# Filter twiddles by one vector product and a sum in PSUM, and a smaller last store, in a long-convolution kernel

## The chip, the cores and the metric

The kernel runs on one core of one Trainium2 chip. The metric is the device time of one execution in microseconds (us). The core has a matrix engine (TensorE, in the profile PE, its weight loads PEld), a vector engine (VectorE, DVE), an activation engine (ScalarE, ACT), GpSimd (POOL) and SyncE (SP), which here only issues transfers. ACT and POOL issue transfers as well. Each engine works through its own instructions in order and waits on semaphores; the transfers run beside them on 16 DMA engines that all queues share.

## The reference, cut to what matters

Batch 4, sequence 12800, width 128, filter order 64, all in float32:

```python
h_filt = (np.maximum(pos_emb @ w1, 0.0) @ w2) * np.exp(-0.01 * pos)[:, None]
u = x * v
y = np.fft.irfft(np.fft.rfft(u, n=2 * S, axis=1) * np.fft.rfft(h_filt, n=2 * S, axis=0)[None], n=2 * S, axis=1)[:, :S]
a = x * y                                   # gated long convolution
gate = 1 / (1 + np.exp(-depthwise_conv5(a)))  # causal, 5 taps
out = (gate * (a @ w_val)) @ w_out
```

The three small weights of the last line come in as float64.

## The kernel before, in words

The convolution of length 25600 is done as a two-step Fourier transform: a position is split into j (2 halves), n1 (100) and n2 (64), and a frequency into k1 (100) and k2 (64). The program has three phases, and each hands its result to the next through device memory.

**Phase 1** (lines 209 to 427) makes two things. The *signal* part is a generator, `signal()`: for each of 64 values of n it multiplies x by v, forms sums and differences on DVE (`prep`, lines 324 to 345, lines 319 to 338 in the profile), transforms over n1 with matmuls (tile `fp`, line 387), copies the result from PSUM to a tile `st` on ACT (line 388), and stores that to the array `a_u` in device memory. It yields after each of the two halves (`c`) of an n, so it has 128 half steps. The inputs come by SP into a ring of nine buffers (`fetch`); when the matmuls of a pair of n have read their buffers, `release` loads them anew. One n reads 0.82 MB and writes 0.82 MB.

The store of an n has three parts by k1 (`PARTS`, line 32): rows k1 = 0 to 63 on the ACT queue, 64 to 95 on the POOL queue (both line 394), and 96 to 99 on the POOL queue one n later (line 407).

The *filter* part is a second generator, `filt()`, with three kinds of step:

- 34 steps that transpose `pos_emb`, multiply by w1 and write the windowed, rectified result to `g_sb` (lines 229 to 254);
- 32 steps `ap` (lines 261 to 272): matmuls that transform `g_sb` over n1, and an ACT copy into `ag`;
- 26 steps `fk`/`gp` (lines 274 to 293): for four k1 at a time, `turned` makes four twiddled 128 x 128 matrices. For each k1, ACT writes sine times one table, and DVE adds cosine times another table to it in place (line 279). A matmul per k1 then multiplies `ag` by the matrix (line 289), and ACT copies the four results back into `ag` (line 291). The first of the 26 steps only makes the first matrices.

The two generators are interleaved by a list of due times, `due` (lines 411 to 414), counted in n; after each half step of the signal, all filter steps that are due are issued. The order in which the lines run is the order in which each engine gets its instructions (`manual_schedule`). Before the change the 34 steps are due from n = 3 on, each half an n apart, to 19.5; the 32 steps from 20 to 36.5; the 26 steps from 36.5 to 63.

**Phase 2** (lines 454 to 589) runs over 50 pairs p of k1 (p holds k1 = 2p and 2p + 1). For each pair the 128 rows of `a_u` at these two k1 are loaded (`load_a`, line 201), transformed over n2 (`z_ps`, line 482), multiplied by the filter's spectrum (`times`, line 488, tiles va, vb, vc, vd on DVE) and transformed back; results go to `c_y` and `c_z`. Pairs 0 and 1 are loaded in pieces: `EARLY` holds the rows of n = 0 to 55, `LATE` those of n = 56 to 63 (line 188). The `EARLY` rows of pair 0 are loaded from the POOL queue at n = 61, and those of pair 1 at n = 63; the `LATE` rows by SP at the start of phase 2. The tiles of phase 2 lie in pools `p2` and `ps2`, in memory that phase 1 held before.

**Phase 3** (lines 599 to 825) finishes the inverse transform, multiplies by x, and does the five taps, the gate and the two projections. The change does not touch it.

Of the kernel before, what the change touches and what calls it, by code (L numbers as in the profile page):

```python
# [9 lines left out]
F32 = mybir.dt.float32  # L10
F32R = mybir.dt.float32r
I32 = mybir.dt.int32
AF = mybir.ActivationFunctionType
ALU = mybir.AluOpType
PSUM = bass.MemoryType.PSUM
# [8 lines left out]
B, S, D, FO, KC = 4, 12800, 128, 64, 5  # L24
J, N1, N2 = 2, 100, 64
# [92 lines left out]
def tile_longconv_gate(  # L118
# [20 lines left out]
    nc = tc.nc  # L139
# [15 lines left out]
    dft = const.tile([128, 2, 2 * N2], F32, name="dft")  # L155
# [53 lines left out]
    with tc.tile_pool(name="p1", bufs=1) as p1, tc.tile_pool(name="ps1", bufs=1, space=PSUM) as ps1:  # L209
        pos_v = pos.rearrange("(j a n) f -> j a n f", j=J, a=N1)  # L210

        g_sb = p1.tile([N1, J, N2, FO], F32, name="g_sb")

        HC = 16

# [8 lines left out]
        def filt():  # L224
# [47 lines left out]
                yield  # L272

            def turned(k0):
                fk = p1.tile([128, 4, 2 * N2], F32, name="fk", bufs=2)
                for i in range(4):
                    k1 = k0 + i
                    nc.scalar.activation(fk[:, i], dft[:, 1], AF.Copy, scale=tw[:, 1, k1:k1 + 1])
                    nc.vector.scalar_tensor_tensor(
                        fk[:, i], dft[:, 0], tw[:, 0, k1:k1 + 1], fk[:, i], op0=ALU.mult, op1=ALU.add)  # L280
                return fk

            fk = turned(0)
# [1 line left out]
            for k0 in range(0, N1, 4):  # L285
                following = turned(k0 + 4) if k0 + 4 < N1 else None
                gz = ps1.tile([128, 4, 2 * N2], F32, name="gp", bufs=1)
                for i in range(4):
                    nc.tensor.matmul(
                        out=gz[:, i], lhsT=ag[:, k0 + i].rearrange("p j e -> p (j e)"), rhs=fk[:, i], start=True, stop=True)  # L290
                nc.scalar.copy(out=ag[:, k0:k0 + 4].rearrange("p k j e -> p k (j e)"), in_=gz)
                fk = following
                yield
# [59 lines left out]
        def signal():  # L353
            fetch(4)
            load_pos(0)
            fetch()
            load_pos(HC)
            ready = [prep(0)]
            for n in range(N2):
                if n == 8:  # L360
                    nc.gpsimd.dma_start(out=dft, in_=t_dft)
                    nc.gpsimd.dma_start(out=tw, in_=t_tw)
                    nc.gpsimd.dma_start(out=inv, in_=t_inv)
                if n == 12:
                    for dst, src in ((wval, w_val), (wout, w_out), (cw, conv_w.rearrange("k d -> d k"))):
                        raw = p1.tile(list(dst.shape), mybir.dt.int64, name=f"raw{len(raws)}")
                        nc.gpsimd.dma_start(out=raw, in_=src)
                        raws.append((dst, raw))
                if n in (18, 22, 26):
                    _narrow(nc, p1, *raws[n // 4 - 4])  # L370
                if n == BACK + 2:
                    load_w(0)
                if n == N2 - 3:
                    for part in EARLY:
                        load_a(0, part, nc.gpsimd)
                if n == N2 - 1:
                    for part in EARLY:
                        load_a(1, part, nc.gpsimd)
                if n + 1 < N2:
                    ready.append(prep(n + 1))  # L380
                both = ready.pop(0)
                st = p1.tile([128, 2, J * BD], F32, name="st", bufs=4)
                for c in range(2):
                    fp = ps1.tile([128, J, BD], F32, name="fp", bufs=2)
                    for j in range(J):
                        h = slice(j * 64, j * 64 + 64)
                        nc.tensor.matmul(out=fp[:, j], lhsT=fsd[h, c], rhs=both[c][h], start=True, stop=True)  # L387
                    nc.scalar.copy(out=st[:, c], in_=fp.rearrange("k j e -> k (j e)"))  # L388
                    yield
                src = st.rearrange("k c e -> k (c e)")  # L390
                row = n % 2 * N2 + n // 2 * 2
                dst = a_u[:, row:row + 2].rearrange("k c e -> k (c e)")
                for eng, (k0, k, step, p0) in zip((nc.scalar, nc.gpsimd), PARTS):
                    eng.dma_start(out=dst[k0:k0 + k], in_=src[p0:p0 + step * (k - 1) + 1:step])  # L394
                if n % 2 == 1:
                    release()
                rest.append((dst, src))
                if len(rest) > 1 or n + 1 == N2:
                    flush()
# [8 lines left out]

        n_done = [False]

        due = [3 + i / 2 for i in range(J * N2 // 4 + 2)]
        for n, w in ((FO // 2, 16.5), (N1 // 4 + 1, 26.5)):
            t0 = due[-1] + 0.5 if n == FO // 2 else t0 + 16.5
            due += [t0 + w * i / n for i in range(n)]
        sig, fil = signal(), filt()
        with tc.manual_schedule():
            for i in range(2 * N2):
# [33 lines left out]
                out=to.rearrange("k (q f) -> k q f", q=2),  # L451
                in_=c_z[k0:k0 + n, m, :, c, n0:n0 + R].rearrange("k q i e -> k q (i e)"))

    with tc.tile_pool(name="p2", bufs=1) as p2, tc.tile_pool(name="ps2", bufs=1, space=PSUM) as ps2:
        half = [slice(h * N2, (h + 1) * N2) for h in range(2)]

        def filter_pair(p):
# [409 lines left out]
```

## Time and profile before

| | |
|---|---|
| median of 3 runs | 1087.39 us (1085.34 to 1089.99) |
| the profiled execution | 1088.63 us, span 1086.8 us |
| phase 1, to the end of the last `st` copy | 328.7 us |
| from there to the first vector product of phase 2 | 13.9 us |
| busy over the span | PE 89%, DVE 90%, ACT 58%, POOL 69% |
| bytes moved by the DMA engines | 330.14 MB, mean 304 GB/s |

The row of the page with the granted TensorE clock in 40 slices reads mostly 9 (90% or more of full speed), with 8 in parts of phase 1 and 6 in the slice of the change of phase. The busy shares are means over three phases with different limits, so they say little of phase 1. What is to be read are stretches: busy time of each engine, granted clock, share of the DMA engines and GB/s between two points in time; then the order of single instructions with the idle time ahead of each and what ended it. In such rows x gives the number of instructions; TensorE runs one float32 matmul of the program as two instructions, so four matmuls of `gp` stand as x8.

### The profile page before, as it was taken

The numbers are of one execution on the slowest core, as the hardware profiler recorded it, in microseconds if no ns is written. First come the engines' busy times: TensorE is split into PE (matmuls) and PEld (weight loads), VectorE is DVE, ScalarE is ACT, GpSimd is POOL, SyncE is SP. The second block draws the span as 40 slices with busy tenths as digits, with TensorE's granted clock in tenths as the row PEclk, the third lists the DMA queues.
The fourth block names the chain that finished last, engine by engine and source line by source line (L and its number), as shares of the span: only waits on it lengthen the run. The fifth ranks groups of instructions, "written<-read, shape, count | busy, mean of one in ns | idle before, by whom it ended". The sixth has DMA issues, their size and how long they took to land. (4 is left out here: it accounts for less than half of the span.)

```text
span 1086.8 us, 21222 instructions
## 1 busy us (share of the span) xinstructions
PE 969.1 (89%) x7880; PEld 489.8 (45%) x7880; DVE 980.7 (90%) x1136; ACT 625.7 (58%) x1017; POOL 749.8 (69%) x469
## 2 busy tenths in 40 slices
PE   2778899877875999999999999689999999999996
PEld 0344466433432554445445555334444444444442
DVE  8869996599983999999999999369999999999997
ACT  1445577687771444444444444266776777767774
POOL 2232322222223999999999999779999999999990
PEclk9989899899886999999999999899999999999999
DMA  8999998898967799998999998886888888888822
GB/s 283 379 351 397 365 335 327 320 353 301 384 237 252 272 338 338 319 343 316 328 329 340 333 337 290 303 321 241 302 278 294 305 278 301 276 294 305 281 82 121
DMA packets 97216, 330.14 MB, mean 304 GB/s; under 512 B 12756, under 2 KB 37948, under 8 KB 81116
## 3 DMA queue, kind: packets, MB, share of 16 engines
q1 hardware_dynamic: 41344, 195.06, 52.9%
q10 hardware_dynamic: 49516, 111.37, 26.5%
q0 software_dynamic: 6256, 22.37, 5.7%
q8 instruction: 64, 1.05, 0.4%
q14 instruction: 36, 0.29, 0.1%
HBM read 197.67 MB, written 131.07 MB: 302 GB/s over the span
## 5 line engine op out<-in xcount | busy, mean ns | idle before, releaser
L682 POOL TENSOR_TENSOR ext<-yr,xr 128x400 f32<-128x400 f32 x120 | 307.7, 2565 | 27.8 <-DVE yr L680 23.3
L699 DVE SCALAR_TENSOR_TENSOR gt<-ext,cw,gt 128x1600 f32<-128x1600 f32 (+1 forms) x132 | 241.6, 1830 | 0.1
L394 POOL DMA_DIRECT2D a_u<-st x64 | 34.3, 536 | 239.0 <-ACT st L388 235.0
L388 ACT COPY st<-fp 128x1024 f32<-128x1024 f32 x128 | 130.6, 1027 | 106.1 <-PE fp L387 53.2
L387 PE MATMUL fp<-ld,fsd 64*128 64x512 f32 x320 | 96.6, 699 | 46.5 <-ACT st L388 19.9
L657 PE MATMUL sd<-ld,inv 128*64 128x512 f32 x512 | 126.6, 613 | 8.1 <-DMA ld<-c_y 7.8
L488 DVE TENSOR_TENSOR va<-z_ps,h_sb 128x2048 f32<-128x2048 f32 x50 | 114.0, 2280 | 21.0 <-PE z_ps L482 20.9
L564 POOL TENSOR_TENSOR va<-va,vb 128x1024 f32<-128x1024 f32 x49 | 116.6, 2380 | 22.1 <-DVE vb L488 22.0
L533 POOL TENSOR_TENSOR c_both<-c_raw 128x512 f32<-128x512 f32 x100 | 126.2, 1288 | 7.0 <-DMA c_z<-c_both 4.4
L526 ACT COPY c_raw<-c_ps 128x1024 f32<-128x1024 f32 x50 | 50.8, 1015 | 134.5 <-PE c_ps L521 127.4
L482 PE MATMUL z_ps<-ld,ld 64*64 64x512 f32 x800 | 112.7, 617 | 14.3 <-DMA ld<-a_u 9.2
L488 DVE TENSOR_TENSOR vb<-z_ps,h_sb 128x2048 f32<-128x2048 f32 x50 | 114.1, 2283 | 10.9 <-POOL va L567 10.9
L662 ACT COPY sd_sb<-sd 128x512 f32<-128x512 f32 x128 | 75.8, 592 | 75.2 <-PE sd L657 63.3
L721 PE MATMUL o_ps<-gd,wout 128*128 128x400 f32 x256 | 111.4, 517 | 8.3 <-DVE gd L716 6.8
L711 PE MATMUL v_ps<-ext,wval 128*128 128x400 f32 x252 | 105.4, 500 | 0.0
L567 POOL TENSOR_TENSOR va<-va,vb 128x1024 f32<-128x1024 f32 x42 | 101.0, 2405 | 0.0
L498 PE MATMUL c_ps<-va,ld 64*64 64x512 f32 x800 | 97.9, 603 | 2.6 <-DVE va L564 1.4
L669 PEld LDWEIGHTS tp<-ident,sd_sb 128*128 128x128 f32 x512 | 58.7, 141 | 77.0 <-PE sd L657 49.6
L669 PE MATMUL tp<-ident,sd_sb 128*128 128x128 f32 x512 | 80.5, 281 | 3.8 <-DVE yr L680 2.7
L504 ACT COPY c_sb<-c_ps 128x1024 f32<-128x1024 f32 x49 | 49.7, 1014 | 57.5 <-PE c_ps L498 57.5
L387 PE MATMUL fp<-xv,fsd 64*128 64x512 f32 x192 | 56.2, 676 | 20.2 <-ACT st L388 8.9
L716 DVE TENSOR_TENSOR gd<-v_ps,sg 128x400 f32<-128x400 f32 x126 | 70.9, 563 | 0.2 <-ACT sg L704 0.2
(109 smaller groups left out, 1763.6 us busy)
## 6 DMA issues: line engine op xcount, KB each, us to landing
ld<-a_u SPq DMA_DIRECT2D x48, 1024.0 KB
a_u<-st ACTq DMA_DIRECT2D x64, 512.0 KB
xr<-in_xt_dram SPq DMA_DIRECT2D x32, 800.0 KB
c_y<-c_sb ACTq DMA_DIRECT2D x49, 512.0 KB
out_dram<-o_sb ACTq DMA_DIRECT2D x31, 800.0 KB
c_z<-c_both ACTq DMA_DIRECT2D x48, 512.0 KB
ld<-in_xv_dram SPq DMA_DIRECT2D x40, 512.0 KB
a_u<-st POOLq DMA_DIRECT2D x64, 256.0 KB, 6.2
```

The costliest lines, as they stand in the source:

```text
L387: nc.tensor.matmul(out=fp[:, j], lhsT=fsd[h, c], rhs=both[c][h], start=True, stop=True)
L388: nc.scalar.copy(out=st[:, c], in_=fp.rearrange("k j e -> k (j e)"))
L482: nc.tensor.matmul(out=z[half[h], c], lhsT=wk[half[c], 0, half[h]], rhs=a2[half[c], h, j], start=True, stop=True)
L488: nc.vector.tensor_tensor(out, z.rearrange("p (b d) -> p b d", d=D).unsqueeze(1).to_broadcast([128, n, B, D]), h_sb.unsqueeze(2).to_broadc ...
L533: nc.gpsimd.tensor_tensor(both[:, :, m], raw[:, :, 1], raw[:, :, 0], op=op)
L564: (nc.gpsimd if nxt else nc.vector).tensor_tensor(va[:, 0:2], va[:, 0:2], vb[:, 0:2], op=ALU.add)
L657: nc.tensor.matmul(out=to, lhsT=inv[:, 2 if j * m * c else c], rhs=t, start=True, stop=True)
L669: nc.tensor.transpose(out=tp[:, b], in_=t[:, b], identity=ident)
L682: nc.gpsimd.tensor_tensor(e[:, r0 + r], yr, xr, op=ALU.mult)
L699: nc.vector.scalar_tensor_tensor(gt, rows(t, k)[:, cols], cw[:, k:k + 1], gt, op0=ALU.mult, op1=ALU.add)
L711: nc.tensor.matmul(out=v_ps, lhsT=wval, rhs=rows(t)[:, r * ROW:(r + 1) * ROW], start=True, stop=True)
L721: nc.tensor.matmul(out=o_ps, lhsT=wout, rhs=gd, start=True, stop=True)
```

## The change

Five edits:

- **The twiddled matrices.** `turned` no longer sums in place. DVE writes cosine times table 0 for four k1 in one operation, with both inputs broadcast; ACT writes sine times table 1 as before, to a place of its own. Their sum is formed in PSUM: two matmuls per k1 instead of one, both with the same stationary operand.
- **Where they lie.** The tile `fk` is gone. The matrices lie in the space of `g_sb` (made 128 rows high and named `g_all`), in four places that are used in turn; before there were two.
- **The due times.** 34 steps over 15.5 n from n = 3, 32 steps over 20 n (18.5 to 38.5), 26 steps over 22 n (38.5 to 60.5).
- **The end of phase 1.** The `EARLY` rows of pairs 0 and 1 are loaded by SP, at n = 58 and 60. The ACT store of the last two n (62 and 63) is cut in two: rows k1 = 0 to 3, which are what pairs 0 and 1 read, then 4 to 63.
- **The pools of phase 2** get `reuse_waits="tile"`: a tile that takes over memory waits for what lay in that memory, and not for the whole of the old pool. Phase 3 has it already.

```diff
-        g_sb = p1.tile([N1, J, N2, FO], F32, name="g_sb")
+        g_all = p1.tile([128, J * N2 * FO], F32, name="g_sb")
+        g_sb = g_all[:N1].rearrange("a (j n e) -> a j n e", j=J, e=FO)
...
             def turned(k0):
-                fk = p1.tile([128, 4, 2 * N2], F32, name="fk", bufs=2)
+                at = k0 % 16 * 256
+                fk = g_all[:, at:at + 1024].rearrange("p (c i e) -> p c i e", c=2, i=4)
                 for i in range(4):
-                    k1 = k0 + i
-                    nc.scalar.activation(fk[:, i], dft[:, 1], AF.Copy, scale=tw[:, 1, k1:k1 + 1])
-                    nc.vector.scalar_tensor_tensor(
-                        fk[:, i], dft[:, 0], tw[:, 0, k1:k1 + 1], fk[:, i], op0=ALU.mult, op1=ALU.add)
+                    nc.scalar.activation(fk[:, 1, i], dft[:, 1], AF.Copy, scale=tw[:, 1, k0 + i:k0 + i + 1])
+                nc.vector.tensor_tensor(
+                    fk[:, 0], dft[:, 0].unsqueeze(1).to_broadcast([128, 4, 2 * N2]),
+                    tw[:, 0, k0:k0 + 4].unsqueeze(2).to_broadcast([128, 4, 2 * N2]), op=ALU.mult)
                 return fk
...
                 for i in range(4):
-                    nc.tensor.matmul(
-                        out=gz[:, i], lhsT=ag[:, k0 + i].rearrange("p j e -> p (j e)"), rhs=fk[:, i], start=True, stop=True)
+                    for c in range(2):
+                        nc.tensor.matmul(
+                            out=gz[:, i], lhsT=ag[:, k0 + i].rearrange("p j e -> p (j e)"), rhs=fk[:, c, i],
+                            start=(c == 0), stop=(c == 1))
...
-                if n == N2 - 3:
+                if n in (N2 - 6, N2 - 4):
                     for part in EARLY:
-                        load_a(0, part, nc.gpsimd)
-                if n == N2 - 1:
-                    for part in EARLY:
-                        load_a(1, part, nc.gpsimd)
+                        load_a((n - N2 + 6) // 2, part)
...
                 for eng, (k0, k, step, p0) in zip((nc.scalar, nc.gpsimd), PARTS):
-                    eng.dma_start(out=dst[k0:k0 + k], in_=src[p0:p0 + step * (k - 1) + 1:step])
+                    cuts = [0, 4, k] if k0 == 0 and n >= N2 - 2 else [0, k]
+                    for a, b in zip(cuts, cuts[1:]):
+                        eng.dma_start(out=dst[k0 + a:k0 + b], in_=src[p0 + step * a:p0 + step * (b - 1) + 1:step])
...
-        due = [3 + i / 2 for i in range(J * N2 // 4 + 2)]
-        for n, w in ((FO // 2, 16.5), (N1 // 4 + 1, 26.5)):
-            t0 = due[-1] + 0.5 if n == FO // 2 else t0 + 16.5
+        due, t0 = [], 3
+        for n, w in ((J * N2 // 4 + 2, 15.5), (FO // 2, 20), (N1 // 4 + 1, 22)):
             due += [t0 + w * i / n for i in range(n)]
+            t0 += w
...
-    with tc.tile_pool(name="p2", bufs=1) as p2, tc.tile_pool(name="ps2", bufs=1, space=PSUM) as ps2:
+    with tc.tile_pool(name="p2", bufs=1, reuse_waits="tile") as p2, \
+            tc.tile_pool(name="ps2", bufs=1, space=PSUM, reuse_waits="tile") as ps2:
```

The instructions stand in a new order at two places. In the changed kernel these lines lie one to four further down (387 is 388, 289 is 292, 338 is 342).

The first place is the stage of the 26 steps, on TensorE. `fp` is the signal's transform (one row x2 is one half step), `gp` the filter step; `ld` and `xv` are the ring's buffers. Before:

```order
L387 MATMUL fp<-ld_75,fsd 128x512 x2
L289 MATMUL gp<-fk,ag 128x128 x4
L387 MATMUL fp<-ld_76,fsd 128x512 x4
L289 MATMUL gp<-fk,ag 128x128 x4
L387 MATMUL fp<-ld_75,fsd 128x512 x2
L387 MATMUL fp<-ld_77,fsd 128x512 x2
```

Now:

```order
L292 MATMUL gp<-g_sb,ag 128x128 x8
L388 MATMUL fp<-ld_76,fsd 128x512 x4
L292 MATMUL gp<-g_sb,ag 128x128 x8
L388 MATMUL fp<-ld_75,fsd 128x512 x2
L292 MATMUL gp<-g_sb,ag 128x128 x8
L388 MATMUL fp<-ld_77,fsd 128x512 x2
```

A filter step holds eight matmuls instead of four, and the steps stand closer: between two of them there is sometimes only one half step of the signal.

On DVE, at the same place, the rows of line 279 (four operations of 128 x 128) become one operation of 128 x 512 in line 280. Before:

```order
L319 TENSOR_TENSOR ld_77<-ld_77 128x1024
L279 SCALAR_TENSOR_TENSOR fk<-dft,tw,fk 128x128 x4
L319 TENSOR_TENSOR ld_78<-ld_78 128x1024
L330 TENSOR_TENSOR ld_77<-ld_77,ld_78 128x1024
L331 TENSOR_TENSOR ld_78<-ld_77,ld_78 128x1024
```

Now:

```order
L323 TENSOR_TENSOR xv_104<-xv_104 128x1024
L280 TENSOR_TENSOR g_sb<-dft,tw 128x512
L323 TENSOR_TENSOR xv_105<-xv_105 128x1024
L334 TENSOR_TENSOR xv_104<-xv_104,xv_105 128x1024
L335 TENSOR_TENSOR xv_105<-xv_104,xv_105 128x1024
```

The operation reads the tables `dft` and `tw` alone, and no longer what ACT wrote just before it.

The second place is the end of phase 1, on SP. The names with `in_xv_dram` are the last input loads; `56x2x1024` are the `EARLY` rows, `8x2x1024` the `LATE` rows, `128x2x1024` whole pairs. Before:

```order
L308 DMA ld_76<-in_xv_dram 32x2048
L308 DMA ld_76<-in_xv_dram 4x2048
L201 DMA ld_80<-a_u 8x2x1024 x2
L201 DMA ld_77<-a_u 8x2x1024 x2
L201 DMA ld_78<-a_u 128x2x1024
```

Now:

```order
L312 DMA ld_76<-in_xv_dram 4x2048
L201 DMA ld_80<-a_u 56x2x1024 x2
L201 DMA ld_77<-a_u 56x2x1024 x2
L201 DMA ld_80<-a_u 8x2x1024 x2
L201 DMA ld_77<-a_u 8x2x1024 x2
L201 DMA ld_78<-a_u 128x2x1024
```

The four `EARLY` loads stand behind the last input load and ahead of the `LATE` loads. On the POOL queue, where they stood ahead of the stores of n = 62 and n = 63, there are now stores alone. On the ACT queue the last rows read as follows.

```order
L389 COPY st<-fp 128x1024 x2
L397 DMA a_u<-st 4x2048
L397 DMA a_u<-st 60x2048
L473 COPY h_sb_2344<-c_ps 128x512
L474 ACTIVATE h_sb_2344<-c_ps 128x2x128
```

The store of four rows goes out ahead of that of sixty, and the `LATE` loads read what the small store wrote.

## The prediction

> **What bounds the kernel now.** I read the stretches first. The first row is the signal with the 34 filter steps (17 to 106.4 us; 106.4 is the 38th of the 128 `st` copies, n = 18.5), the second the last of the 34 steps and the `ap` stage, the third the `fk`/`gp` stage to the end of the last copy, the fourth the seam, the fifth most of phase 2. The columns are busy us (count) of PE, PEld, DVE, ACT and POOL, then granted clock, DMA share, GB/s.
>
> ```profile
> 17.00:106.40 89.40, 66.71 (x332) 33.95 (x330) 74.19 (x95) 42.80 (x53) 23.32 (x41) 0.92 1.00 370
> 106.40:200.40 94.00, 88.16 (x666) 56.25 (x668) 73.30 (x106) 65.88 (x69) 23.58 (x38) 0.96 0.93 342
> 200.40:328.70 128.30, 95.42 (x418) 48.03 (x414) 118.31 (x203) 94.64 (x180) 32.62 (x58) 0.89 0.86 317
> 328.70:342.60 13.90, 4.69 (x38) 2.10 (x42) 0.00 (x0) 1.14 (x3) 1.89 (x4) 0.62 0.74 204
> 342.60:675.00 332.40, 326.14 (x4640) 168.78 (x4638) 321.86 (x193) 144.41 (x237) 316.74 (x178) 0.98 0.92 325
> ```
>
> Four different limits: the transfers (share 1.00) in the first row; PE (88.2 of 94 us) in the second; DVE (118.3 of 128.3 us) in the third, with PE at 95.4 and its clock at 0.89; nobody in the fourth. Phase 2 is bound by DVE again. So two things are open to this change: the imbalance of the second and third rows, and the seam. The waits between 200 and 328 us, and the copies by stretch:
>
> ```profile
> DVE fk L279 <- ACT fk L278: 21.4, 2, 20.7
> PE fp L387 <- issue: 4.7, 1, 4.7
> 106.40:200.40 94.00, 38.17 (x36) 0.96 0.93 342
> 200.40:328.70 128.30, 55.48 (x55) 0.89 0.86 317
> ```
>
> DVE once stood 20.7 us ahead of its first `fk`, waiting for ACT, which came to it only after the last `ap` copy; when DVE resumed, PE starved 4.7 us for the next signal. 36 + 55 = 91 half steps fall into the two stretches.
>
> **The change, part by part.** *TensorE from n = 18.5 on.* Rows of both stages:
>
> ```profile
> 172.90 0.65 PE L265 MATMUL ap<-fwd,g_sb 100*64 100x200 f32 x4
> 174.33 1.13 PE L387 MATMUL fp<-ld,fsd 64*128 64x512 f32 x4
> 175.39 0.65 PE L265 MATMUL ap<-fwd,g_sb 100*64 100x200 f32 x4
> 282.81 1.16 PE L289 MATMUL gp<-fk,ag 128*128 128x128 f32 x8
> 283.90 1.99 PE L387 MATMUL fp<-ld,fsd 64*128 64x512 f32 x8
> ```
>
> From start to start a half step costs 1.06 us (174.33 to 175.39), an `ap` step 1.43 (172.90 to 174.33), a `gp` step 1.09 (282.81 to 283.90). The new `gp` step has twice the matmuls of the same shape, each with its own weight load: I price it at 2.18. Then 91 x 1.06 + 32 x 1.43 + 25 x 2.18 = 96.5 + 45.8 + 54.5 = 196.8 us. Begun at 106.4, PE without a gap ends at 303.2.
>
> *VectorE.* The nearest rows to the new 128 x 512 product are these, the second with an operand broadcast along its last axis:
>
> ```profile
> L338 DVE TENSOR_TENSOR ld<-ld 128x512 f32<-128x512 f32 x80 | 52.1, 687 | 0.7
> L251 DVE SCALAR_TENSOR_TENSOR g_sb<-gp,win 100x512 f32<-100x512 f32 x16 | 11.0, 685 | 13.0 <-PE gp L231 13.0
> 282.17 1.13 DVE L279 SCALAR_TENSOR_TENSOR fk<-dft,tw,fk 128x128 f32<-128x128 f32 x4
> 283.22 0.68 DVE L338 TENSOR_TENSOR ld<-ld 128x512 f32<-128x512 f32 x1
> 283.83 0.68 DVE L338 TENSOR_TENSOR xv<-xv 128x512 f32<-128x512 f32 x1
> ```
>
> Four `fk` take 1.05 us from start to start, one 128 x 512 operation 0.61; both bounds of the new price are 0.69. 25 x 0.44 = 11 us less, and the two stretches' 73.3 + 118.3 = 191.6 us become 181: DVE would be done by 287 and is no longer the bound. The product also waits for no ACT row, so the restart after the last `ap` is earlier; the 4.7 us of starving PE should shrink, since two half steps that DVE has prepared already and the first `gp` step stand ahead of the next one that it still has to make. ACT's 65.9 + 94.6 = 160.5 us stay and hide behind PE.
>
> *Transfers.* The two stretches moved 94.0 x 342 + 128.3 x 317 = 32.1 + 40.7 = 72.8 MB. At the 370 GB/s of the full row that is 196.8 us: the same 303.2. Two budgets that meet leave no room for either to lag.
>
> *What is lost on top.* (a) Collisions: in the `ap` row PE was idle 5.8 of 94 us although it was the bound; I take 6. (b) The tail: the last 3.5 n (7 half steps) have no filter step, so PE's 1.06 is not the pace; at DVE's 118.3 - 25 x 1.05 = 92 us over 55 half steps, 1.67, the most is 4.3; DVE will be ahead, so 3. (c) The clock. These rows show that it falls with gaps:
>
> ```profile
> 150.00:200.00 50.00, 50.00 (x404) 32.96 (x402) 30.79 (x35) 38.61 (x41) 11.10 (x20) 1.00 0.91 330
> 205.00:235.00 30.00, 23.30 (x96) 11.82 (x96) 29.08 (x47) 20.53 (x41) 6.41 (x12) 0.83 0.90 327
> 265.00:295.00 30.00, 22.78 (x102) 11.94 (x102) 29.79 (x52) 22.93 (x47) 6.98 (x13) 0.89 0.97 374
> ```
>
> A PE that is busy all the time has 1.00, one that is busy 23 of 30 us has 0.83 to 0.89. The `gp` stage now asks for 25 x 2.18 + 42 x 1.06 = 99 us of PE over 21 n. At 1.00 the loss is 0, at 0.89 it is 99 x (1/0.89 - 1) = 12; a nearly full stage is nearest to the first row, so 3. The Trainium skill, page "TensorE: Matmul & The Clock Gate", section "Part 1: The HAM clock gate", says that the clock is halved after an idle window of some 3.4 us and restored after as long a busy one. By that rule a stage without gaps loses nothing and the time is 3 us less; with 0.89 kept it is 9 us more. The three rows agree with the rule.
>
> Sum: 303.2 + 12 = 315.2 for the end of the last copy, against 328.7. Gain 13.5; between 3 (303.2 + 12 clock + 6 + 4.3) and 25 (no loss).
>
> *The 34 steps in 15.5 n* cost nothing: there the transfers are full, and PE (66.7) and DVE (74.2 of 89.4) have room. Were DVE full there, the products that now come before n = 18.5 (two of the 16) would add 1.4 us there.
>
> *The seam.* Rows from the ACT queue, POOL, SP, PE and DVE:
>
> ```profile
> 326.12 0.46 ACTq L394 DMA_DIRECT2D a_u<-st  x1
> 326.75 1.93 ACT L388 COPY st<-fp 128x1024 f32<-128x1024 f32 x2 [0.66 <-PE fp L387]
> 327.50 1.35 POOL L201 DMA_DIRECT2D ld<-a_u  x2
> 328.71 0.46 ACTq L394 DMA_DIRECT2D a_u<-st  x1
> 329.13 0.30 SPq L201 DMA_DIRECT2D ld<-a_u  x1
> 337.62 0.28 SPq L201 DMA_DIRECT2D ld<-a_u  x1
> 340.54 1.12 PE L482 MATMUL z_ps<-ld,ld 64*64 64x512 f32 x2 [1.03 <-DMA ld<-a_u]
> 342.61 2.29 DVE L488 TENSOR_TENSOR va<-z_ps,h_sb 128x2048 f32<-128x2048 f32 x1 [20.92 <-PE z_ps L482]
> ```
>
> Call 328.7 T. The store of n = 62 (issued 326.12) released SP's first `LATE` load 3.0 us later; that of n = 63 (328.71) released the second only after 8.9, with POOL's `EARLY` loads of pair 1 (issued 327.50) moving at the same time. Then 2.9 us to the matmul, 2.1 to DVE: 13.9 in all. In the change the `EARLY` loads are gone from there, and the load waits for a store of 32 KB. I price it by the unjammed 512 KB store, 3.0 us (above that 8.9; below it the issue's 0.46). T + 3.0 + 2.9 + 2.1 = T + 8.0: gain 5.9, between 0 and 8. SP's next load, of pair 2, waits for the 60-row store; pair 2's product is due two pairs later, 2 x 332.4 / 50 = 13 us, so that is covered. The page "DMA: Bandwidth & Descriptors" of the Trainium skill, section "Anatomy of one DMA", gives some 2.0 us of fixed cost per transfer. By that the small store takes 2.1 us and the time is 0.9 less.
>
> The tile-wise waits of the new pools cost nothing and are what lets that happen: before, the first ACT copy of phase 2 waited for all of phase 1:
>
> ```profile
> ACT h_sb L469 <- DMA ld<-a_u: 9.6, 1, 9.6
> ```
>
> **Sum.** 13.5 + 5.9 = 19.4 us. The profiled execution's own 1088.63 - 19.4 = 1069.2; it stood 1.2 above the median of the runs, so 1068, and I say 1069 since two equal budgets rather err late. Phases 2 and 3 only start earlier.
>
> **Rivals.** *Transfers set the pace.* For it: 1.00 in the first row, and equal budgets. Against: the 342 and 317 GB/s of the second and third rows are what PE and DVE asked for, not what the transfers could give, and the input loads end up to nine n (the ring's buffers) before the last copy, after which only stores run. At 342 GB/s, 72.8 MB take 213 us: 319.3, with the tail 322.3; 6.4 + 5.9 = 12.3 gained, 1075.
>
> *The seam keeps its wait,* because a POOL store or another semaphore comes last: 13.5 gained, 1074.
>
> *The clock stays at 0.89:* 9 us more, 1077. With the full collisions as well, 1083, which is no change.
>
> *Slower.* The second matmul of a pair adds to the same PSUM place as the first; if it must wait for the first to land, each of 100 costs x more. To end 0.5% (5.4 us) above before in spite of the seam's 5.9, the last copy must come at 328.7 + 5.9 + 5.4 = 340, 25 us beyond 315.2: from x = 0.25 us on, on a matmul of 0.27, the change loses. Against: the two pieces of one float32 matmul (x8 for four) already follow each other in 1.09 / 8 = 0.14 us. Time from 1093 up.
>
> **Chances and range.** Forecast 0.60 (1061 to 1075); transfers 0.19; seam 0.07; clock 0.09; slower 0.05. With 0.5% (about what a measurement of this kernel tells from no change) the line is at 1082: faster 0.87 (forecast, transfers, seam and most of the clock's), same 0.08, slower 0.05. The range 1059 to 1081 goes from nearly no loss to the transfers' and clock's cases.
>
> **What would show it.** After: the `ap` stage still PE-bound but nearer 4.5 us per n, the `gp` stage with PE near full, clock over 0.95 and DVE with gaps; the `gp` rows at 2.2 us per x16; the 128 x 512 products at 0.69; the last copy near 315; DVE's first product some 8 us behind it. A DMA share of 0.97 and more from 106 us on speaks for the transfers, `gp` rows over 3 us for the slow rival. A last copy after 326 would prove the main term wrong.

## The result

The changed kernel took 1073.57 us (median of 4 runs, 1064.47 to 1075.18) beside 1088.69 us for the kernel before (4 runs): ratio 0.9846, 95% interval 0.9815 to 0.9877, so 1.2 to 1.9% faster. Run once more beside the experiments it took 1070.11 us (6 runs) beside 1087.50: ratio 0.9831, interval 0.9790 to 0.9872. Forecast were 1069 us and a range of 1059 to 1081.

The profiled execution of the change has a span of 1070.4 us. These are its stretches, cut at the same events as those shown of before: the first 38 copies, the end of the `ap` stage, the `gp` stage and the tail to the end of the last copy, the seam, most of phase 2 (busy us and count of PE, PEld, DVE, ACT, POOL; clock, DMA share, GB/s).

```profile
17.00:109.60 92.60, 68.57 (x346) 36.13 (x342) 75.70 (x91) 43.05 (x54) 25.99 (x43) 0.91 1.00 365
109.60:204.00 94.40, 88.39 (x668) 56.06 (x670) 83.13 (x120) 68.86 (x73) 23.31 (x41) 0.96 0.96 364
204.00:314.10 110.10, 99.98 (x618) 63.37 (x614) 98.75 (x119) 91.09 (x177) 27.88 (x50) 1.00 0.93 349
314.10:324.35 10.25, 4.05 (x22) 1.60 (x26) 0.00 (x0) 1.15 (x4) 1.69 (x3) 0.56 0.64 193
324.35:659.70 335.35, 324.55 (x4624) 172.32 (x4620) 321.26 (x192) 144.46 (x237) 316.02 (x178) 0.99 0.91 322
```

The first stretch is 3.2 us longer than before (92.6 against 89.4), the third 18.2 us shorter with PE's clock at 1.00 instead of 0.89, the seam 10.25 us instead of 13.9. The second and third stretch do not hold the same work in both kernels, since the `ap` stage now ends two n later: 41 and 51 copies instead of 36 and 55. So these two lengths are not a gain by stage; the table of events below is. The prices, from the timeline and from the groups of instructions of the change:

```profile
254.78 2.05 PE L292 MATMUL gp<-g_sb,ag 128*128 128x128 f32 x16 [0.82 <-ACT ag L295]
256.76 1.56 PE L388 MATMUL fp<-ld,fsd 64*128 64x512 f32 x6
```
```profile
L280 DVE TENSOR_TENSOR g_sb<-dft,tw 128x512 f32<-128x512 f32 x25 | 16.9, 685 | 9.7 <-PE ap L266 9.7
```

A `gp` step takes 1.98 us from start to start (forecast 2.18), the new product 0.69 us as forecast. Now the seam of the change, from the ACT queue, SP, PE and DVE:

```profile
310.39 1.62 ACTq L397 DMA_DIRECT2D a_u<-st  x2
312.18 1.93 ACT L389 COPY st<-fp 128x1024 f32<-128x1024 f32 x2 [1.82 <-PE c_ps L467]
314.14 1.47 ACTq L397 DMA_DIRECT2D a_u<-st  x2
317.57 0.27 SPq L201 DMA_DIRECT2D ld<-a_u  x1
322.27 1.12 PE L486 MATMUL z_ps<-ld,ld 64*64 64x512 f32 x2 [1.77 <-DMA ld<-a_u]
324.35 2.29 DVE L492 TENSOR_TENSOR va<-z_ps,h_sb 128x2048 f32<-128x2048 f32 x1 [19.68 <-PE z_ps L486]
```

The last copy ends at 312.18 + 1.93 = 314.1 (T). The small store, issued at 314.14, lets SP's load go at 317.57 (3.4 us); the load takes 4.7 us to the matmul at 322.27; DVE starts 2.1 us later: T + 10.2. From the rows of both kernels:

| event | before, us | change, us | gain |
|---|---|---|---|
| 38th copy starts | 106.3 | 109.6 | -3.3 |
| VectorE has made its last product of phase 1 | 321.7 | 304.7 | 17.0 |
| last copy ends | 328.7 | 314.1 | 14.6 |
| first product of phase 2 | 342.6 | 324.35 | 18.3 |
| last pair's product | 680.9 | 666.4 | 14.5 |
| end of the span | 1086.8 | 1070.4 | 16.4 |

Up to the first product the gain is 18.3 us, against 19.4 forecast. Phase 2 then took 3.8 us more in this execution (last part of the experiments).

**Who was late.** One can keep an account for VectorE: the start of the 38th copy, plus its work until its last product of phase 1, plus its idle time. Here is that stretch, and below it 42 copies of the steady `gp` stage, first of before and then of the change:

```profile
106.30:321.70 215.40, 178.08 (x1063) 101.77 (x1064) 191.71 (x309) 156.68 (x245) 53.88 (x92) 0.93 0.89 332
214.20:309.50 95.30, 71.96 (x332) 36.97 (x331) 94.52 (x164) 75.28 (x147) 23.33 (x42) 0.93 0.90 336
```
```profile
109.60:304.70 195.10, 183.16 (x1252) 117.79 (x1252) 181.87 (x238) 154.18 (x243) 48.19 (x86) 0.98 0.95 358
205.30:300.40 95.10, 89.63 (x556) 59.21 (x557) 93.24 (x113) 81.68 (x166) 23.41 (x42) 1.00 0.93 354
```

Before: 191.7 us of work and 23.7 idle. Change: 181.9 and 13.2. Of the 17.0 us that VectorE ends sooner, 9.8 are work, 10.5 are idle time (nearly all the one wait ahead of the first filter matrix, 20.7 us before and 9.7 after), and 3.3 are lost at the start. The steady stage has the same length in both (95.3 and 95.1 us for 42 copies), and VectorE is busy 99% and 98% of it; in the change some 24 filter steps fit in, before some 20. The stretch ahead of it, which holds the wait, is 12.2 us shorter (107.9 to 95.7 us), the last eight copies behind it are 5.5 us shorter (19.2 to 13.7 us). So the shorter wait and the shorter tail carry the gain, and VectorE didn't get the gaps that I had forecast.

### The profile page after: what moved, and what is told of

Same layout as the page of the kernel before. It is cut to its first block, busy times and chain, and to the rows that moved or that the text cites. A ratio compares the mean times of both kernels' runs of the same rounds, so it can differ in the third digit from the quotient of the medians.

```text
span 1070.4 us, 21514 instructions
## 1 busy us (share of the span) xinstructions
PE 973.9 (91%) x8080; PEld 510.3 (48%) x8080; DVE 972.7 (91%) x1061; ACT 625.9 (58%) x1017; POOL 747.4 (70%) x465
## 5 line engine op out<-in xcount | busy, mean ns | idle before, releaser
L703 DVE SCALAR_TENSOR_TENSOR gt<-ext,cw,gt 128x1600 f32<-128x1600 f32 (+1 forms) x132 | 255.1, 1932 | 0.1
L388 PE MATMUL fp<-ld,fsd 64*128 64x512 f32 x320 | 88.6, 656 | 30.7 <-ACT st L389 15.6
L720 DVE TENSOR_TENSOR gd<-v_ps,sg 128x400 f32<-128x400 f32 x126 | 84.2, 669 | 0.2 <-ACT sg L708 0.2
L683 DVE TENSOR_TENSOR yr<-tp,dif 128x204 f32<-128x204 f32 x128 | 58.8, 459 | 23.9 <-ACT dif L675 23.8
```

The lines of the kernel that those rows point to most:

```text
L703: nc.vector.scalar_tensor_tensor(gt, rows(t, k)[:, cols], cw[:, k:k + 1], gt, op0=ALU.mult, op1=ALU.add)
```

## The experiments

All ran beside the kernel before. T is the end of the last copy, the seam is from T to DVE's first product of phase 2, both from each kernel's profile; the ratio is to the kernel before.

| kernel | median, us | ratio, 95% interval | T | seam |
|---|---|---|---|---|
| before | 1087.5 to 1088.7 | | 328.7 | 13.9 |
| changed kernel | 1073.6 | 0.9846 (0.9815 to 0.9877) | 314.1 | 10.2 |
| changed_again | 1070.1 | 0.9831 (0.9790 to 0.9872) | 314.0 | 9.8 |
| sums_only | 1071.4 | 0.9851 (0.9819 to 0.9884) | 314.3 | 13.4 |
| due_only | 1093.6 | 1.0058 (1.0031 to 1.0085) | 331.7 | 15.5 |
| seam_only | 1082.0 | 0.9958 (0.9933 to 0.9984) | 329.6 | 9.2 |
| no_seam | 1073.5 | 0.9867 (0.9836 to 0.9898) | 312.4 | 15.6 |
| old_spans | 1070.6 | 0.9838 (0.9798 to 0.9879) | 313.5 | 9.9 |
| four_products | 1071.2 | 0.9842 (0.9795 to 0.9888) | 313.5 | 9.8 |
| chained | 1082.6 | 0.9957 (0.9924 to 0.9989) | 324.6 | 9.8 |
| less_input | 1068.6 | 0.9832 (0.9781 to 0.9882) | 313.2 | 10.3 |
| one_matmul | 1068.3 | 0.9825 (0.9781 to 0.9868) | 310.7 | 10.1 |
| early_only | 1068.6 | 0.9828 (0.9775 to 0.9881) | 315.4 | 9.7 |
| late_first | 1066.9 | 0.9821 (0.9777 to 0.9865) | 314.7 | 8.5 |

### One part of the change at a time

**sums_only**: before, with the new matrices and the sum in PSUM alone.

```diff
-                fk = p1.tile([128, 4, 2 * N2], F32, name="fk", bufs=2)
+                fk = g_all[:, at:at + 1024].rearrange("p (c i e) -> p c i e", c=2, i=4)
...
+                    for c in range(2):
+                            start=(c == 0), stop=(c == 1))
```

> The kernel before with the new matrices alone (one VectorE product per four k1 and the sum in PSUM, in the rotating places); old step spans, old seam. My theory: until about 200 us nothing changes; then the last stage needs 118.3 - 11 = 107 us of VectorE and 55 x 1.06 + 25 x 2.18 = 113 us of PE over its 26.5 n, so PE takes over and with the losses the last copy ends at 318 to 321 instead of 328.7; seam 13.9 as before; time 1079 to 1082, gain 7 to 10. Rival A (the new spans are the whole gain, the old thin spread hides the new matrices): last copy 327 to 329, time 1087 to 1090. Rival B (the added matmuls cost more than VectorE gives back): slower than 1090.

T came at 314.3: the whole gain of phase 1, with the old step spans. My theory had the direction and only two thirds of the size, rival A falls. Its account, its steady stage and its wait:

```profile
106.70:307.60 200.90, 187.36 (x1253) 117.74 (x1253) 180.05 (x234) 154.99 (x244) 52.04 (x89) 0.98 0.93 351
210.30:299.90 89.60, 84.69 (x511) 53.54 (x510) 88.89 (x108) 74.91 (x147) 23.31 (x42) 1.00 0.97 371
```
```profile
DVE g_sb L280 <- PE ap L266: 18.6, 1, 18.6
```

Work 180.05 (11.7 less than before), idle 20.8, end at 307.6 instead of 321.7. By this account it is VectorE's work that counts with the old spans: 11.7 of the 14.1 us. The long wait is still there, only for another reason: the product writes into the space of the filter's first stage, and waits for the last `ap` matmul that reads it. In the steady stage PE, VectorE and the transfers are all nearly full (84.7 and 88.9 of 89.6 us, share 0.97).

**due_only**: before, with the new step spans alone.

```diff
-        due = [3 + i / 2 for i in range(J * N2 // 4 + 2)]
...
+        for n, w in ((J * N2 // 4 + 2, 15.5), (FO // 2, 20), (N1 // 4 + 1, 22)):
```

> The kernel before with the new step spans alone; old matrices (four VectorE operations per four k1, one matmul per k1). My theory: the PE-bound ap stage gets 20 n instead of 16.5 and runs at some 94 us for its 40 copies; the gp stage is then bound by VectorE, 42 half steps x 1.67 + 26 x 1.05 = 96.4 us plus collisions of 3 to 8 us; last copy 317 to 322, time 1080 to 1083. So each of the two edits alone would give well over half of the 14.6 us that both give, because before the two stages were unequal and either edit evens them out. Rival A (VectorE, whose 191.6 us of work are not cut, stays the bound of the whole): last copy 326 to 329, time 1087 to 1089.

Slower, by 0.3 to 0.9%: my theory fell, and rival A was still too kind. The account, the steady stage and the wait:

```profile
109.20:326.80 217.60, 177.06 (x1062) 102.77 (x1064) 194.98 (x313) 154.72 (x244) 50.60 (x89) 0.91 0.86 323
206.50:316.50 110.00, 77.32 (x356) 42.05 (x356) 101.43 (x180) 81.06 (x167) 23.31 (x42) 0.91 0.83 303
```
```profile
DVE fk L279 <- ACT fk L278: 20.2, 5, 12.8
```

The first 38 copies come 2.9 us later, VectorE's work is not less, and its idle time (22.6) neither: what the first wait lost (12.8 instead of 20.7) came back as waits for ScalarE inside the stage, where 42 copies now take 110 us with nobody full. I had added up work and had forgotten that in the old form each matrix is handed from ScalarE to VectorE.

**old_spans**: the changed kernel, with the old step spans (the reverse of the last diff). **changed_again**: the changed kernel.

> The changed kernel with the old step spans (34 steps half an n apart, 32 over 16.5, 26 over 26.5); matrices and seam as changed. From the run with the matrices alone (last copy 314.3, as the changed kernel's 314.1, in spite of the old spans) I now expect the same last copy, 312 to 316, a seam of 9.2 to 10.5, and 1067 to 1071, 2 to 4 us ahead of the changed kernel, since the first 38 copies come 3 us sooner and the earlier loads take no POOL time. Rival: the new spans carry the seam's gain and without them it is lost at the store queue; 1071 to 1075.

> The changed kernel itself once more, beside the others on the same chip: whether its 1073.6 over four runs holds. Its profiled execution had a phase 2 of 342.0 us from first to last pair, where five other profiles had 335.7 to 338.9. If that was chance, the median falls to 1068 to 1071 and the profile's phase 2 is under 340; if the edits make phase 2 stall more, the median stays at 1073 to 1075 and phase 2 near 342.

1070.6 and 1070.1 us, T 313.5 and 314.0, seams 9.9 and 9.8: the new spans are worth nothing that can be measured once the matrices are new. What they gain (VectorE idle 19.4 with the old ones, 12.3 with the new) they give back at the start (106.3 against 109.5), in work that is left after it (179.9 against 182.8) and in the distance from VectorE's end to T (7.8 against 9.5). The advantage that I expected of old_spans did not show either.

**seam_only** and **no_seam**: before with the seam's three edits, and the change without them.

```diff
-                if n == N2 - 3:
+                if n in (N2 - 6, N2 - 4):
                     for part in EARLY:
-                        load_a(0, part, nc.gpsimd)
+                        load_a((n - N2 + 6) // 2, part)
...
+                    cuts = [0, 4, k] if k0 == 0 and n >= N2 - 2 else [0, k]
...
+    with tc.tile_pool(name="p2", bufs=1, reuse_waits="tile") as p2, \
```

> The kernel before with the seam's edits alone (loads of the first two pairs earlier and on SP, small store first, tile-wise pool waits). My theory: last copy at 328.7 as before; first product of phase 2 10 us behind it instead of 13.9, as in the changed kernel; time about 1085, gain 3 to 5. Rival: before, transfers have room near the end (share 0.5 to 0.75), so the seam is nearer the 8.0 that I predicted; gain 6, 1082. Second rival: the earlier loads hold SP's input loads back, last copy later than 330 and no gain.

> The changed kernel with the old seam (loads of the first two pairs on the POOL queue at the end, whole stores, old pools); new matrices and new spans stay. My theory: last copy 313 to 316, seam 13.9, time 1075 to 1079: 3 to 5 us behind the changed kernel. Rival: phase 1's gain needs the POOL queue free of those loads; last copy over 318 and time over 1080.

seam_only: 5.7 us less, seam 9.2: the rival's time, and a seam between the two theories. no_seam: seam 15.6, T 312.4 and 1073.5 us, all three outside of what I expected; it is 3.4 us behind the changed kernel's second median, though against the first there is no difference. Old seams were 13.4 to 15.6, new ones 9.2 to 10.3. A part of that is taken back ahead of T: with the seam's edits the last copy comes 0.9 us later in the old kernel (329.6 against 328.7) and 1.7 us later in the new one (314.1 against 312.4). So the first product of phase 2 gains 3.8 us in the old kernel (342.6 to 338.8) and 3.6 us in the new one (328.0 to 324.35).

### Work or waiting

**four_products**: the changed kernel, with the product made in four pieces.

```diff
-                nc.vector.tensor_tensor(
-                    fk[:, 0], dft[:, 0].unsqueeze(1).to_broadcast([128, 4, 2 * N2]),
+                for i in range(4):
+                    nc.vector.tensor_tensor(
+                        fk[:, 0, i], dft[:, 0], tw[:, 0, k0 + i:k0 + i + 1].to_broadcast([128, 2 * N2]), op=ALU.mult)
```

> The changed kernel, but the 128x512 VectorE product per four k1 is made as four 128x128 products, none of which reads what ScalarE writes. VectorE gets its 25 x about 0.4 = 10 us back; that its operation waits for no ScalarE result stays as in the change. Theory 1 (the gain of phase 1 is VectorE time, as my prediction put it): the last copy goes back from 314 by most of it, to 320 to 325, time 1079 to 1085. Theory 2 (the gain is the broken chain ScalarE, VectorE, PE, ScalarE within a gp step, which took about 4.2 us per step whatever stood between): last copy 312 to 317, time 1070 to 1076.

```profile
L281 DVE TENSOR_TENSOR g_sb<-dft,tw 128x128 f32<-128x128 f32 x100 | 22.0, 282 | 10.0 <-PE ap L266 10.0
```
```profile
108.00:308.30 200.30, 186.04 (x1264) 118.71 (x1264) 187.94 (x313) 156.41 (x245) 50.62 (x89) 0.97 0.94 360
```

T 313.5 and 1071.2 us, as theory 2 said. But the test was weaker than planned: the pieces cost 22.0 us instead of 16.9, so 5 us and not 10, and VectorE's end moved from 304.7 to 308.3 while its distance to T shrank from 9.4 to 5.2. The changed kernel has some 4 us of room there; that VectorE's work had no part in the gain does not follow, and sums_only shows that it had.

**chained**: the changed kernel, with the product reading ScalarE's output.

```diff
-                    fk[:, 0], dft[:, 0].unsqueeze(1).to_broadcast([128, 4, 2 * N2]),
+                    fk[:, 0], fk[:, 1],
```

> The changed kernel, but the one 128x512 VectorE product reads ScalarE's four results of the same step in place of the first table, so that it must wait for them (the filter computed is another one: the cosine part is replaced by the product of both twiddles with the second table). VectorE's time, PE's and the transfers stay. Theory 1 (VectorE time): last copy 312 to 317, time 1070 to 1076. Theory 2 (the chain): last copy 320 to 330, time 1078 to 1090.

T 324.6 and 1082.6 us: 10.6 us of T for a wait, with the same instructions on each engine. Its account and steady stage, its wait, and one step of its timeline (ACT, PE and DVE):

```profile
107.40:319.10 211.70, 187.94 (x1264) 119.05 (x1264) 183.74 (x238) 156.37 (x245) 50.55 (x89) 0.98 0.91 340
204.80:310.80 106.00, 90.61 (x552) 58.86 (x552) 92.26 (x111) 82.32 (x167) 23.41 (x42) 1.00 0.89 321
```
```profile
DVE g_sb L280 <- ACT g_sb L279: 25.6, 10, 13.8
```
```profile
262.65 1.93 ACT L389 COPY st<-fp 128x1024 f32<-128x1024 f32 x2 [0.48 <-PE fp L388]
264.46 1.28 ACT L279 ACTIVATE g_sb<-dft,tw 128x128 f32<-128x128 f32 x4
265.77 0.69 DVE L280 TENSOR_TENSOR g_sb<-g_sb,tw 128x512 f32<-128x512 f32 x1 [2.08 <-ACT g_sb L279]
266.38 1.22 DVE L323 TENSOR_TENSOR xv<-xv 128x1024 f32<-128x1024 f32 x1
```

ScalarE makes its four results only behind the copies that stand ahead of them, and those wait for PE. VectorE stands 2.08 us for it, and behind its product stands the signal's next one (266.38), which has nothing to do with ScalarE. 42 copies take 106.0 us instead of 95.1. So with the new spans the product's independence is worth some 10 us; with the old spans, where fewer steps fall into the stage, the same hand-over cost one wait of 20.7 us and hardly anything after it (VectorE 94.5 of 95.3 us busy in before). A kernel with the old spans and this product chained was not run.

### What holds T at 314 now

**less_input** and **one_matmul**: the changed kernel, the first with 13 MB less to load, the second with one matmul per k1.

```diff
-                for k0, k, step, p0 in PARTS:
+                for k0, k, step, p0 in PARTS if n < 20 else PARTS[:1]:
```
```diff
-                    for c in range(2):
-                        nc.tensor.matmul(
-                            out=gz[:, i], lhsT=ag[:, k0 + i].rearrange("p j e -> p (j e)"), rhs=fk[:, c, i],
-                            start=(c == 0), stop=(c == 1))
+                    nc.tensor.matmul(
+                        out=gz[:, i], lhsT=ag[:, k0 + i].rearrange("p j e -> p (j e)"), rhs=fk[:, i % 2, i],
+                        start=True, stop=True)
```

> The changed kernel, but from the 21st signal matrix on only 64 of its 100 rows are loaded (the others hold what is left in the buffer, so the products are others): 44 x 36 rows x 8 KB = 13 MB less for the transfers, 35 us at 370 GB/s; every engine's instructions stay. In six kernels with the new matrices the last copy came at 312.4 to 314.3, though VectorE was done anywhere from 304.6 to 308.3: something else holds the end. Theory 1 (transfers): last copy 306 to 311, where VectorE's own end plus 5 stands. Theory 2 (PE): 312 to 315. Theory 3 (both budgets are equal, as my prediction had it: taking one away leaves the other): 311 to 314.

> The changed kernel with one matmul per k1 instead of two (half of the terms of the filter's sum are left out; both matrices are still made): 25 x 1.09 = 27 us less PE, all else stays. Theory 1 (transfers hold the end at 314): last copy 312 to 315. Theory 2 (PE holds it): 306 to 311. Theory 3 (equal budgets): 311 to 314.

The steady stage of less_input, then that of one_matmul, and a step of one_matmul's PE:

```profile
204.95:299.80 94.85, 92.03 (x570) 60.12 (x568) 93.95 (x114) 83.47 (x169) 23.32 (x42) 1.00 0.86 307
```
```profile
205.90:297.80 91.90, 71.71 (x366) 38.80 (x367) 91.18 (x111) 80.15 (x167) 23.32 (x42) 0.98 0.96 371
```
```profile
252.55 1.58 PE L291 MATMUL gp<-g_sb,ag 128*128 128x128 f32 x8 [3.21 <-DVE g_sb L280]
```

With 307 GB/s instead of 354 the stage is as long as before (94.85 against 95.1), T some 0.8 us earlier: the transfers alone don't set the pace, theory 1 falls. Theories 2 and 3 both allow for 313.2. With PE at 72 instead of 90 us of the stage, T comes at 310.7, 3.4 us earlier, and PE now waits for VectorE, which is busy 91.2 of 91.9 us. That number lies in theory 2's range, but only 0.3 us outside of theory 3's, and of the some 18 us taken from PE only 3.4 arrive. So VectorE stands right behind PE. The transfers are not far either: they move 371 GB/s at a share of 0.96 there, the rate of the full first stretch. Which of the three would come next is not shown. Neither time differs from the changed kernel's by more than the intervals allow.

### The seam's parts

**early_only**: the changed kernel with whole stores and the old pools. **late_first**: the changed kernel with the last 60-row store behind the load.

```diff
+                        if a and n == N2 - 1:
+                            for part in LATE:
+                                load_a(0, part)
+                            eng = nc.sync
                         eng.dma_start(
...
-                        for part in LATE:
+                        for part in LATE if q else ():
```

> The changed kernel with whole stores and the old pool waits; of the seam's edits only the earlier loads on SP are left. If these are the whole gain, as my prediction's equal price for the small store and the unjammed large one says: first product 9.2 to 10.5 us behind the last copy. If the small store matters: 11 to 13, since the load then waits for 512 KB among the other last stores. If the tile-wise waits matter, the first ScalarE copy of phase 2 comes after all stores have landed (some 8 us behind the last copy) and VectorE waits for it instead of for PE: 10.5 to 13.

> The changed kernel with the last 60-row store (480 KB) issued by SP behind the two last loads of pair 0, instead of by ScalarE ahead of them. In the changed kernel the load took 4.7 us from its issue to the matmul, against 2.9 before; if the large store ahead of it is the cause, 3 us and a seam of 8 to 8.8, time 1 to 2 us less; if not (the POOL stores, or a fixed delay), 9.2 to 10.5.

Of early_only, the end of the ACT queue, SP's load, PE, ACT's first copy of phase 2 and DVE:

```profile
313.43 1.93 ACT L389 COPY st<-fp 128x1024 f32<-128x1024 f32 x2 [0.66 <-DMA a_u<-st]
315.39 0.46 ACTq L395 DMA_DIRECT2D a_u<-st  x1
320.11 0.26 SPq L201 DMA_DIRECT2D ld<-a_u  x1
321.56 0.58 ACT L470 COPY h_sb<-c_ps 128x512 f32<-128x512 f32 x1 [6.20 <-DMA a_u<-st]
322.97 1.12 PE L483 MATMUL z_ps<-ld,ld 64*64 64x512 f32 x2 [0.55 <-DMA ld<-a_u]
325.05 2.29 DVE L489 TENSOR_TENSOR va<-z_ps,h_sb 128x2048 f32<-128x2048 f32 x1 [17.35 <-PE z_ps L483]
```

Seam 9.7: the earlier loads are the whole gain. The whole store releases the load after 4.7 us instead of 3.4, but the load then takes 2.9 us (320.11 to 322.97) instead of 4.7, since nothing of 480 KB stands ahead of it. ACT's first copy waits 6.2 us for the stores, as with the old pools, and is done over 2 us before DVE needs it. The split has a price besides: its second issue holds ACT (1.62 us for two against 0.46 for one), and the idle time ahead of the last two copies is 1.82 us in the changed kernel and 0.66 here. T is no earlier for it (315.4).

The earlier loads have a price ahead of T. These are ACT's waits for stores among the last eight copies, first of the change and then of early_only:

```profile
ACT st L389 <- DMA a_u<-st: 2.5, 2, 1.6
```
```profile
ACT st L389 <- DMA a_u<-st: 1.7, 2, 1.0
```

A copy writes into one of four `st` buffers and has to wait until the store of what lay there has landed. no_seam, which lacks the earlier loads and is otherwise nearest to early_only, has no such wait in its last eight copies, and its T is 312.4 against 315.4. So the loads probably slow the last stores; this rests on one profile of each kernel.

Of late_first, the small store, SP's load, PE's weight load behind that load, and DVE:

```profile
314.73 0.62 ACTq L401 DMA_DIRECT2D a_u<-st  x1
318.57 0.27 SPq L201 DMA_DIRECT2D ld<-a_u  x1
321.11 0.18 PEld L490 LDWEIGHTS z_ps<-ld,ld 64*64 64x64 f32 x2 [1.70 <-DMA ld<-a_u]
323.20 2.29 DVE L496 TENSOR_TENSOR va<-z_ps,h_sb 128x2048 f32<-128x2048 f32 x1 [17.48 <-PE z_ps L490]
```

The load takes 2.5 us (318.57 to 321.11) instead of 4.7, as expected, the small store 3.8 instead of 3.4; the seam is 8.5, the shortest of all. With 1066.9 us it has the lowest median here, but its interval covers the changed kernel's; a version surely better than the change has not been shown.

### Phase 2, which nobody edited

First to last pair took 338.3 us before (342.61 to 680.87) and 342.0 in the change (324.35 to 666.39). The same in the other profiles: 335.7 (seam_only) to 340.8 (changed_again), in kernels with the old pools 338.2 to 340.6. DVE's waits in phase 2, of before, of the change and of seam_only:

```profile
DVE vb L488 <- POOL va L567: 10.5, 14, 2.1
```
```profile
DVE vb L492 <- POOL va L571: 13.4, 14, 2.5
```
```profile
DVE vb L488 <- POOL va L567: 8.0, 14, 1.7
```

Fourteen waits in each, whose lengths differ from one execution to the next, with no order by the edits. My expectation that changed_again would stay under 340 was missed by 0.8 us, its median came as expected. What makes these waits longer or shorter is open. Between the change and before they make 2.9 of the 3.8 us; over all profiles phase 2 spreads by 6.3 us (335.7 to 342.0), and so far one execution can differ from another without the edits having a part in it.

## Why the prediction was right, and where it was not

- **The end of phase 1** (315.2 forecast, 314.1 measured) is right by errors that cancel. Start: 106.4 forecast, 109.6 measured; "the 34 steps in 15.5 n cost nothing" was wrong by 3.2 us. PE's work: 196.8 forecast; between the 38th copy and T the two stretches hold 88.4 + 100.0 = 188.4 us. Losses: 12 forecast, and 204.5 - 188.4 = 16.1 idle. Together that is 3.2 - 8.4 + 4.1 = -1.1 us; that they cancel so nearly is luck.
- **PE's new price** was near: 1.98 us a step against 2.18. The slower rival (a matmul that waits for the one before it in the same place) falls: 16 follow each other in 2.05 us, 0.13 us each.
- **VectorE's 11 us** were right in size (9.8, and 11.7 in sums_only). The step that failed is the one behind it, "DVE would be done by 287 and is no longer the bound". It counted 106.4 + 181 and no idle time. The first product still waits (9.7 us, and 18.6 with the old spans), now for PE's last `ap` matmul; VectorE ends at 304.7 and is full in the `gp` stage. The forecast gaps did not appear.
- **The wait for ScalarE** was seen, but priced only through PE's 4.7 us of starving. Put back into the changed kernel (chained) the hand-over costs 10.6 us of T. This is the part of the mechanism that the prediction mentioned and did not size. The 10.5 us by which VectorE's idle time fell from before to the change are another thing: with the new matrices and the old spans VectorE was still idle for 20.8 us (sums_only), since the wait for PE's last `ap` matmul took the place of that for ScalarE. Only the new spans brought it down, and they lost as much elsewhere. How much of the gain of sums_only is work and how much is the hand-over rests on the account alone.
- **The new spans** stood in the forecast as what evens out two stages. Alone they lose 0.3 to 0.9%, with the new matrices they change nothing. The sum did not notice, since it went over both stages together. The `ap` stage took 94.4 us for its 20 n, 4.7 us per n where 4.5 was forecast.
- **Transfers** do not set the pace: 13 MB less moved T by 0.8 us, and the rival falls with that; the share of 0.96 and 0.93 had already stayed under the 0.97 that was to speak for it. That they are a second budget beside PE's is neither shown nor refuted, since with equal budgets, too, less to load leaves T in place. VectorE, which the prediction had taken out of the count, is full in the `gp` stage.
- **The clock**: the loss of 3 was too much. The `gp` stage ran at 1.00, though PE was busy 89.6 of 95.1 us, not all of it. Of the rule of the Trainium skill, page "TensorE: Matmul & The Clock Gate", section "Part 1: The HAM clock gate", the forecast said that it gives 3 us less for this term. The change agrees with that: PE's longest idle time from 204 to 314 us is 2.1 us. The rows of before agree less well than the prediction says. There the clock fell to half behind 3.4 us in which PE was busy for 1.64 us, and the idle time that began just before them was 2.75 us long:

```profile
270.70:274.10 3.40, 1.64 (x9) 0.92 (x10) 3.37 (x8) 2.10 (x4) 1.11 (x2) 1.00 1.02 419
274.10:277.50 3.40, 3.40 (x12) 1.89 (x12) 3.40 (x8) 2.53 (x7) 0.00 (x0) 0.50 1.01 423
272.46 1.13 PE L387 MATMUL fp<-xv,fsd 64*128 64x512 f32 x4 [2.75 <-ACT st L388]
```

- **The seam**: 8.0 forecast, 10.2 measured (9.2 to 10.3 over all kernels with the edits). The mis-sized term is the load, 2.9 forecast and 4.7 measured, behind the 480 KB that the same edit puts ahead of it; the store, 3.0 forecast, took 3.4. The fixed 2.0 us of the page "DMA: Bandwidth & Descriptors" of the Trainium skill, section "Anatomy of one DMA", would have made the store 2.1; the measured 3.4 decides. That section is about transfers that GpSimd issues, and ScalarE issues this one. The large store that was to stand for the small one took 4.7 without POOL's loads beside it (early_only), not 3.0. "The tile-wise waits cost nothing" holds; that they "are what lets that happen" does not (early_only).
- **The tail**: the last eight copies take 314.1 - 300.4 = 13.7 us, 5.2 more than PE's 8 x 1.06; 3 were forecast. The split stores hold ACT for 1.2 us of it, and 2.5 us are the two waits for stores. What paces the rest is not settled, nor why VectorE's end stands 5 to 9.5 us ahead of T. A place for the matrices outside the filter's first buffer, which might shorten the last wait of 9.7 us, was not tried.

## What to carry to other kernels

When one engine hands a half-made result to another and both work through their queues in order, price the hand-over as an account of the second engine (start, work, idle to its end), and not only its instructions: behind the waiting instruction stood work that had no part in it. Here it helped to let each engine write its own half and let PSUM add, since PE had room for the second matmul. And before work is spread anew over a phase, ask for each stage who is full in it: with the hand-over still there the same spreading made the kernel slower.

## What was not expected of the hardware

PE's busy time grew by far less than the added matmuls were priced at. Between the 38th copy and T PE was busy 188.4 us in the change and 183.6 before (88.2 + 95.4): 4.8 us more, where 25 x 1.09 = 27 us had been priced. The groups of both kernels over the whole span, first before, then the change:

```profile
L387 PE MATMUL fp<-ld,fsd 64*128 64x512 f32 x320 | 96.6, 699 | 46.5 <-ACT st L388 19.9 <-DVE ld L338 14.8 <-DMA xv<-in_xv_dram 6.3
L289 PE MATMUL gp<-fk,ag 128*128 128x128 f32 x200 | 33.6, 318 | 1.5 <-DVE fk L279 1.0 <-ACT ag L291 0.5
```
```profile
L388 PE MATMUL fp<-ld,fsd 64*128 64x512 f32 x320 | 88.6, 656 | 30.7 <-ACT st L389 15.6 <-DVE ld L342 15.0
L292 PE MATMUL gp<-g_sb,ag 128*128 128x128 f32 x400 | 51.3, 281 | 3.3 <-ACT ag L295 3.3
```

Twice the filter matmuls take 51.3 us instead of 33.6, each 281 ns instead of 318, and the signal's, as many as before, fall from 699 to 656 ns, while the granted clock of the third stretch rises from 0.89 to 1.00. It looks as if a fuller PE paid for part of its own work, but one_matmul, which has the added matmuls out again, says otherwise. From the 38th copy to T its row is this:

```profile
109.15:310.65 201.50, 170.94 (x1088) 98.80 (x1088) 182.85 (x238) 158.19 (x249) 52.09 (x92) 0.97 0.95 364
```

Against it the added matmuls cost 188.4 - 170.9 = 17.5 us, less than 27 but not 4.8. The other part, 183.6 - 170.9 = 12.7 us, came without them: about as many matmul instructions as before (1088 and 1084), in a kernel whose clock stood at 0.97 instead of 0.96 and 0.89. Nor was PE's share of the steady stage the reason: 71.7 of 91.9 us in one_matmul at a clock of 0.98, 72.0 of 95.3 before at 0.93. How the idle time is spread may be, and that was not followed up.
